# A soft-MoE tail in quarters of the output columns instead of halves

## The chip, the cores and the metric

The kernel runs on one core of a Trainium2 chip. The metric is the device time of one launch, in microseconds (us). TensorE is written PE in the profile (PEld for its weight loads), VectorE DVE, ScalarE ACT, GpSimd POOL, and SP is the engine that here issues all DMAs.

## The reference

A linear-attention block (8 batches, 8 heads, 576 tokens, 64 channels) feeds a soft mixture of experts. The change is in the last stage of the second part, so that part is quoted; `x` is the attention's output, 4608 tokens by 512 columns, with 8 experts of 4 slots each and a hidden width of 1024.

```
logits = x @ phi                              # 4608 x 32
d = softmax of logits over the tokens
slot_input = (d.T @ x).reshape(8, 4, 512)
for e in range(8):
    h = relu(slot_input[e] @ w1[e])           # 4 x 1024
    slot_out[e] = h @ w2[e]                   # second layer, 4 x 512
c = softmax of logits over the 32 slots
return c @ slot_out.reshape(32, 512)          # 4608 x 512, float32
```

All inputs and outputs are float32. The output is 9.44 MB; w1 and w2 are 16.8 MB each.

## The kernel before, in words

The attention part takes most of the time and is the same in both kernels; a planner (class `Plan`) sets the order of its work. Behind it everything that PE does is written out by hand, inside `tc.manual_schedule(engines={PE})`; the other engines take their instructions in the order in which a scheduler puts them.

SP loads the 64 tiles of expert weights (512 KB each, `load_w`, L235) into slots of SBUF as these come free, the 32 tiles of w2 last. They are ordered by half `a` of the output columns: 16 tiles (two for each expert) for columns 0 to 255, then 16 for 256 to 511. Behind the last weights SP issues the output DMAs, in order.

The names of the tail, each with its function:

- `hp` (L810) is the first layer, `hidden`/`picked` apply the ReLU (`hs`, L864 on ACT and L865 on DVE) and turn it around (`psh`, L873) into `sh`, the stationary operand of the second layer.
- `layer2(a, e)` (L907) is the second layer of expert `e` for half `a`: eight matmuls, one for each 128 of the hidden width, each with 32 stationary columns (the 32 slots, those of other experts being zero) and 256 moving columns of w2. Four of them go to four groups of 32 PE columns side by side. The sums of all experts stand in `yp`, one PSUM bank for each half. A float32 matmul shows as two instructions in the trace, so one call makes 16.
- `slots(a)` (letter `s`) copies `yp` to `ys` on DVE; `slots2` (`r`, for the second half `R`) adds up the four groups by one matmul with `rep` (`psy`, L920), and ACT and DVE split the result into a pair of rounded parts, `yr` (L923).
- `combine(i)` (`C`) makes the moving operand of 512 tokens' outputs: four transposes on PE (`psc`, L893), a copy on ACT (L897) and a subtraction on DVE (L898) to `cT[i]`. The first three of nine are made earlier, under the names `psc` L604 and `xT`. `psc` and `psy` share two PSUM buffers (`pd`).
- `output(a, i, yr)` (`o`) makes 512 tokens of a half: two matmuls of 512 moving columns (`pso`, L931), one for each 128 output columns, one evicted by DVE and the other by ACT (L932) into a tile `o`, and one DMA of 512 KB (L933). `pso` rotates over four PSUM banks.

The string `TAIL` sets the order of these on PE, one letter a step; `L` is half an expert of the second half of the columns. All of half 0's second layer stands ahead of `TAIL`, and the nine outputs of half 1 behind it.

Of the kernel before, what the change touches and what calls it, by code (L numbers as in the profile page):

```python
# [9 lines left out]
F32 = mybir.dt.float32  # L10
F32R = mybir.dt.float32r
AF = mybir.ActivationFunctionType
ALU = mybir.AluOpType
# [3 lines left out]
B, H, S, D = 8, 8, 576, 64  # L17
# [11 lines left out]
DM, NE, SPE, FF = 512, 8, 4, 1024  # L29
NS = NE * SPE  # L30
KC = DM // 128
FC = FF // 128
SP, PE, ACT, DVE, POOL = (getattr(mybir.EngineType, n) for n in ("SP", "PE", "Activation", "DVE", "Pool"))
NTT = B * S // 128
DH = DM // 2
# [5 lines left out]
NCT = 3  # L41
# [79 lines left out]

TAIL = "CCLLrLLoLLCoLLCoLLCoLLCoLLoLoLsoRo"


@with_exitstack
def tile_kernel(ctx: ExitStack, tc, xT, vv, w, phi, w1, w2, cst, out):
# [7 lines left out]
    nc = tc.nc  # L136
# [44 lines left out]
    for i in range(NWARM):  # L181
        ps = pmm.tile([128, 512], F32, tag="mm", name="psw")
# [9 lines left out]
    cs = const.tile([128, 257], F32, name="cs")  # L192
    ident = cs[:, 0:128]
    rep = cs[:, 128:256]
    low4 = cs[:, 256:257]
# [23 lines left out]
    keep = [10, 11, 12, 13]  # L219
    order = [j for j in range(nslot[-1]) if j not in keep]  # L220
    wt = []
    wpools = [wpool]

    def slot(j, name, dt=F32):
        return wpools[sum(j >= n for n in nslot)].tile([128, 1024], dt, tag=f"w{j}", name=name)
# [372 lines left out]
    cT = []  # L598
# [39 lines left out]
    for s in range(NK):  # L638
        u, c = divmod(s, NCH)
        bp, h = divmod(u, H)  # L640
        n = bp, c
# [6 lines left out]
        bank = [f"kb{s % 2}"]  # L648
# [8 lines left out]
        bank = [f"qb{s % 2}"]  # L657
# [148 lines left out]
    def layer1(a, kcs):  # L806
        for kc in kcs:
            for n in range(2):
                for e in range(4):
                    nc.tensor.matmul(hp[a][32 * e:32 * e + 32, n], si[:, kc],  # L810
                                     wt[(a * KC + kc) * 4 + e][:, n * 512:(n + 1) * 512],
                                     start=kc == 0, stop=kc == KC - 1, skip_group_check=True)
# [27 lines left out]
    def bank(shape, name):  # L840
        cps.append(cps.pop(0))
        return cps[-1].tile(shape, F32, tag="nm0" if cps[-1] is pmo else "mo", name=name)

    def lastw():
        for c in range(NCH):
            n = NBP - 1, c
            ps = bank([128, CH, NS], "psL")
            turned(lTs.pop(n), ps)
            l = sm.tile([128, CH, NS], F32, tag="ls", name="ls", bufs=3)
            nc.vector.tensor_copy(l, ps)  # L850
            wmax(n, l)
            wsub(n, nc.vector)
            wexp(n)
            wsum(n)
            wdiv(n, nc.vector)

    sh = []
# [4 lines left out]
    def hidden(a):  # L862
        t = slot(keep[a], "hs")
        nc.scalar.activation(t[:, 0:512], hp[a][:, 0], AF.Relu, scale=rs)  # L864
        nc.vector.tensor_scalar(t[:, 512:1024], hp[a][:, 1], rs, 0.0, op0=ALU.mult, op1=ALU.max)  # L865
        return t

    def picked(a, t):
        for i in range(2):
            ps = bank([128, FC // 2, 4, NS], "psh")  # L870
            for c in range(FC // 2):
                o = (FC // 2 * i + c) * 128
                nc.tensor.transpose(ps[:, c].rearrange("p e s -> p (e s)"), t[:, o:o + 128], ident)  # L873
            for e in range(4):
                c0 = (4 * a + e) * SPE
                nc.vector.tensor_copy(sh[a][:, e, FC // 2 * i:FC // 2 * (i + 1), c0:c0 + SPE], ps[:, :, e, c0:c0 + SPE])


    spare = [order[i] for i in range(len(wsrc) - nslot[-1], len(order)) if order[i] < NE * KC]
    gone = [i if i < nslot[-1] else order[i - nslot[-1]] for i in range(NE * KC, NE * (KC + 2))]  # L880
    cws, cts = [], []

    def repeated(i):

        if i % 2:
            cws.append(slot(spare[6 + i // 2 - 1], "cw").rearrange("p (g m) -> p g m", g=2))
        cw = cws[-1][:, 1 - i % 2].rearrange("p (j a s) -> p j a s", a=4, s=NS)
        nc.gpsimd.tensor_copy(cw, call[:, 4 * i:4 * i + 4].unsqueeze(2).broadcast_to([128, 4, 4, NS]))

    def combine(i):  # L890
        ps = pd.tile([128, 4, 128], F32, tag="c", name="psc")
        for j in range(4):
            nc.tensor.transpose(ps[:, j], cws[(i - NCT) // 2][:, 1 - i % 2, j * 128:(j + 1) * 128], ident)  # L893
        if i % 2:
            cts.append(slot(spare[i // 2 - 1], "cT", F32R).rearrange("p (g m) -> p g m", g=2))
        x, ps = cts[-1][:, 1 - i % 2], ps.rearrange("p j m -> p (j m)")
        nc.scalar.copy(x, ps)  # L897
        nc.vector.tensor_tensor(x[64:128], ps[64:128], x[64:128].bitcast(F32), op=ALU.subtract)  # L898
        cT.append(x)


    yp = ph[0].tile([128, 2, 512], F32, tag="h", name="yp")

    def layer2(a, e, cs=range(FC)):
        for c in cs:
            g = 32 * (c % 4)
            nc.tensor.matmul(yp[g:g + 32, a, 0:DH], sh[e // 4][:, e % 4, c],  # L907
                             wt[NE * KC + (a * NE + e) * 2 + c // 4][:, (c % 4) * DH:(c % 4 + 1) * DH],
                             start=(e == 0 and c < 4), stop=(e == NE - 1 and c >= 4), skip_group_check=True)

    def slots(a):
        ys = slot(spare[3 + a], "ys")[:, 0:DH]
        nc.vector.tensor_copy(ys, yp[:, a, 0:DH])
        return ys

    yrs = slot(spare[5], "yr", F32R)

    def slots2(a, ys):
        ps = pd.tile([128, DH], F32, tag="c", name="psy")
        nc.tensor.matmul(ps, rep, ys, start=True, stop=True)  # L920
        yr = yrs[:, DH * a:DH * a + DH]

        yis = [nc.scalar.copy(yr, ps), nc.vector.scalar_tensor_tensor(yr, yr.bitcast(F32), low4, ps, op0=ALU.mult, op1=ALU.add)]  # L923
        return yr, yis[0].ins, yis[-1].ins

    def output(a, i, yr):

        o = slot(gone[i] if a == 0 else (gone[9:16] + keep[0:2])[i], "o").rearrange("p (b t) -> p b t", b=2)
        for b in range(2):
            ps = bank([128, 512], "pso")  # L930
            nc.tensor.matmul(ps, yr[:, b * 128:(b + 1) * 128], cT[i], start=True, stop=True)  # L931
            (nc.scalar.copy if b else nc.vector.tensor_copy)(o[:, b], ps)  # L932
        nc.sync.dma_start(out[a, i], o.rearrange("p b t -> p (b t)"))  # L933

    NO = NTT // 4
    with tc.manual_schedule(engines={PE}):
        layer1(1, range(0, 1))
        lastw()
        layer1(1, range(1, 2))
        picked(0, hidden(0))  # L940
        layer1(1, range(2, KC))
        layer2(0, 0)
        layer2(0, 1)
        picked(1, hidden(1))
        stacks["h"].close()
        pd = ctx.enter_context(tc.tile_pool(name="pd", bufs=2, space=PSUM, reuse_waits="tile"))
        for i in range(NCT, NO):
            repeated(i)
        for e in range(2, NE):
            layer2(0, e)  # L950
        ys = slots(0)
        cs, outs, l2 = iter(range(NCT, NO)), iter(range(NO)), iter(range(2 * NE))
        behind = ExitStack()
        for step in TAIL:
            if step == "L":
                e, i = divmod(next(l2), 2)
                layer2(1, e, range(4 * i, 4 * i + 4))
            elif step == "C":
                combine(next(cs))
            elif step == "o":  # L960
                output(0, next(outs), yr)
            elif step == "s":
                ys = slots(1)
            elif step == "r":
                yr, *_ = slots2(0, ys)
            else:
                yr2, *ins = slots2(1, ys)
                for x in ins:
                    behind.enter_context(tc.issue_after(x))
        behind.close()  # L970
        for i in range(NO):
            output(1, i, yr2)


# [32 lines left out]
```

## Time and profile before

| | us |
|---|---|
| median of 3 runs (355.0 to 357.64) | 356.8 |
| the profiled execution | 356.55 |
| its span, first to last instruction | 354.6 |
| PE busy in the span | 340.3 (96%) |
| DVE, ACT, POOL busy | 261.2, 247.0, 168.8 |
| written to HBM | 9.44 MB |

The profiled execution took 1.95 us more than its span. The tail that the change touches begins at 312.7 us, with the first matmul of the second layer.

### The profile page before, as it was taken

Reading aid. Unit: us, or ns where it says so; the run is one execution under the profiler, and the core shown is the slowest. Engines: PE = TensorE matmul, PEld = TensorE weight load, DVE = VectorE, ACT = ScalarE, POOL = GpSimd, SP = SyncE. Lnnn points to the kernel's source line nnn. Section 1 sums busy time; section 2 is a strip of 40 time slices with the busy share of each in tenths; the row PEclk is TensorE's granted clock in tenths of the full one; section 3 lists DMA queues with packets and bytes.
Section 4 is the critical chain, followed back from the end, with each engine's and each line's share of the span. In section 5 each row is a group of like instructions: output and inputs, shape, how many; then the busy total and the mean of one; then the engine's idle time right before and its main releaser. Section 6 shows DMA issues by size and latency. Waiting matters only on the chain.

```text
span 354.6 us, 16589 instructions
## 1 busy us (share of the span) xinstructions
PE 340.3 (96%) x6901; PEld 277.7 (78%) x6901; DVE 261.2 (74%) x762; ACT 247.0 (70%) x840; POOL 168.8 (48%) x356
## 2 busy tenths in 40 slices
PE   8999999999999989999999999999999999999980
PEld 4899989998898879888888998889899755455440
DVE  1678888888889777889897887997887644614680
ACT  3798899869867978788679878877887351203460
POOL 1546666753473756544747674557475400230000
PEclk9999999999999999999999999999999999999996
DMA  6646567535526655545266565344431998997698
GB/s 211 204 137 204 171 209 242 174 108 205 183 57 217 204 190 168 167 143 190 53 210 226 176 206 166 130 165 127 149 99 28 357 414 312 414 415 323 250 409 350
DMA packets 22074, 74.13 MB, mean 209 GB/s; under 512 B 2928, under 2 KB 3184, under 8 KB 22000
## 3 DMA queue, kind: packets, MB, share of 16 engines
q1 hardware_dynamic: 22000, 73.08, 59.2%
q8 instruction: 54, 0.88, 1.0%
q14 instruction: 20, 0.16, 0.1%
HBM read 63.64 MB, written 9.44 MB: 206 GB/s over the span
## 4 chain that ended last, share of the span: by engine, by line
PE 88%; ACT 5%; DVE 3%; issue 1%; POOL 0%; ACTq 0%; DVEq 0%; POOLq 0%
PE kvp L310 20%; PE psn L367 19%; PE psk L266 12%; PE psq L266 9%; PE psx L700 5%; PE yp L907 4%; PE hp L810 4%; PE psl L412 4%; PE pso L931 2%; PE pss L446 2%; PE psw L183 1%; ACT o L932 1%; PE psc L893 1%; ACT kf L292 1%; ACT mh L344 1%
## 5 line engine op out<-in xcount | busy, mean ns | idle before, releaser
L285 POOL TENSOR_TENSOR vs<-vt,mk 128x390 f32<-128x390 f32 (+3 forms) x128 | 91.8, 729 | 63.3 <-PE kvp L310 25.7
L310 PE MATMUL kvp<-vs,kf 128*64 128x65 f32 (+1 forms) x2304 | 92.4, 229 | 1.1 <-issue 1.1
L367 PE MATMUL psn<-kvs,qf 128*64 128x65 f32 x2304 | 85.1, 224 | 1.2 <-ACT qf L336 0.5
L310 PEld LDWEIGHTS kvp<-vs,kf 128*64 128x64 f32 x2304 | 79.2, 138 | 6.9 <-issue 3.3
L367 PEld LDWEIGHTS psn<-kvs,qf 128*64 128x64 f32 x2304 | 75.8, 138 | 8.9 <-issue 1.6
L266 PE MATMUL psk<-wd,xs 64*128 64x128 f32 x576 | 81.5, 284 | 0.0
L266 PE MATMUL psq<-xs,wd 64*128 64x128 f32 x576 | 81.2, 284 | 0.0
L266 PEld LDWEIGHTS psk<-wd,xs 64*128 64x128 f32 x576 | 69.1, 187 | 8.2 <-issue 3.1
L266 PEld LDWEIGHTS psq<-xs,wd 64*128 64x128 f32 x576 | 69.0, 187 | 2.0 <-ACT qf L336 1.0
L332 ACT ACTIVATE qf<-psq 128x384 f32<-128x384 f32 (+2 forms) x96 | 46.2, 484 | 25.3 <-PE psq L266 13.2
L272 DVE TENSOR_REDUCE mk<-psk 128x3 f32<-128x384 f32 (+2 forms) x96 | 51.5, 542 | 15.3 <-PE psk L266 11.3
L326 DVE TRANSPOSE_TENSOR_REDUCE mt<-psq 128x12 f32<-128x384 f32 (+2 forms) x96 | 53.8, 569 | 7.2 <-ACT qf L336 3.5
L292 ACT ACTIVATE kf<-psk 128x384 f32<-128x384 f32 (+2 forms) x96 | 45.9, 486 | 9.8 <-DVE mk L272 8.3
L402 POOL TENSOR_TENSOR xc<-un,dn 128x192 f32<-128x192 f32 x96 | 47.0, 506 | 11.2 <-DVE dn L394 6.3
L336 ACT ACTIVATE qf<-psq 128x384 f32<-128x384 f32 (+2 forms) x96 | 46.2, 483 | 0.1
L296 ACT ACTIVATE kf<-psk 128x384 f32<-128x384 f32 (+2 forms) x96 | 45.7, 488 | 0.0
L378 DVE TENSOR_TENSOR un<-psn,eq 128x195 f32<-128x195 f32 x96 | 32.7, 346 | 11.4 <-PE psn L367 8.3
L383 DVE TENSOR_TENSOR un<-psn,un 128x195 f32<-128x195 f32 x96 | 32.8, 353 | 1.7
L350 DVE TENSOR_REDUCE eq<-mh 32x9 f32<-32x36 f32 x128 | 26.5, 207 | 8.9 <-ACT mh L344 6.8
L344 ACT ACTIVATE mh<-mt 32x36 f32<-32x36 f32 x128 | 29.2, 228 | 3.6 <-DVE mt L326 2.3
L276 ACT ACTIVATE mk<-mk 128x3 f32<-128x3 f32 (+2 forms) x96 | 19.9, 209 | 4.2 <-DVE mk L272 3.2
L700 PE MATMUL psx<-cs,xc 128*128 128x128 f32 x135 | 19.7, 282 | 0.0
(124 smaller groups left out, 355.4 us busy)
## 6 DMA issues: line engine op xcount, KB each, us to landing
wt<-w SPq DMA_DIRECT2D x64, 512.0 KB, 6.8
xs<-xT SPq DMA_DIRECT2D x32, 576.0 KB, 4.1
vt<-vv SPq DMA_DIRECT2D x32, 325.0 KB, 3.1
out<-o SPq DMA_DIRECT2D x18, 512.0 KB, 3.2
xs<-xT SPq DMA_DIRECT2D x1, 160.0 KB, 3.1
cs<-cst SPq DMA_DIRECT2D x1, 128.5 KB, 3.8
xs<-xT SPq DMA_DIRECT2D x1, 128.0 KB, 3.1
wd<-w SPq DMA_DIRECT2D x1, 64.0 KB, 2.7
```

The source lines that it names most:

```text
L266: nc.tensor.matmul(ps, a, b, start=True, stop=True)
L272: nc.vector.tensor_reduce(km[s][:, 2, 0:n], kx[s][:, 0:n], axis=AX, op=ALU.max, apply_absolute_value=True)
L285: nc.gpsimd.tensor_tensor(x[:, :, o:o + n], v[:, t:t + n].unsqueeze(1).broadcast_to([128, 2, n, 65]), em[:, 0:2, i:i + n].unsqueeze(3).bro ...
L292: nc.scalar.activation(kf[s][:, 1, 0:n], kx[s][:, 0:n], AF.Exp, scale=-1.0)
L296: nc.scalar.activation(kf[s][:, 0, 0:n], kx[s][:, 0:n], AF.Exp)
L310: nc.tensor.matmul(ps[f:f + FE // 2, pn, o:o + m], k2[:, pn, i, f:f + FE // 2], v2[:, pn, 65 * i:65 * i + m], start=(t == 0 and pn == 0), ...
L326: nc.vector.tensor_reduce(mts[u].rearrange("p r j -> p j r")[:, t:t + n], qx[s][:, 0:n * 128].rearrange("p (j t) -> p j t", t=32), axis=AX ...
L332: nc.scalar.activation(qf[s][:, 0, 0:n], qx[s][:, 0:n], AF.Exp)
L336: nc.scalar.activation(qf[s][:, 1, 0:n], qx[s][:, 0:n], AF.Exp, scale=-1.0)
L367: nc.tensor.matmul(ps[64 * f:64 * f + 64, j, pn], q2[:, pn, o + 64 * f:o + 64 * f + 64], kv[:, pn, b2], start=True, stop=True)
L402: nc.gpsimd.tensor_tensor(xc[bp, c][:, :, h * D:(h + 1) * D], un[u][:, t, 0:64], dn[u][:, t].unsqueeze(2).broadcast_to([128, CH, 64]), op= ...
L700: nc.tensor.transpose(ps[:, o], xc[n][:, j, kc * 128:(kc + 1) * 128], ident)
```

## The change: what it does

The second layer and the outputs go by quarters of 128 columns (`q` = 0 to 3). A call of `layer2(q, e)` has as many matmuls as before, with 128 moving columns each, so the second layer has 512 matmul instructions where it had 256. Quarters 0 and 1 both read the 16 weight tiles of the first half, quarters 2 and 3 those of the second; `yp` holds two quarters at a time. `L` is now a whole expert of a quarter. There are four `s` and four `r` steps, with 128 columns each. `output(q, i, yr)` makes one matmul of 512 tokens and one eviction, by DVE where `q + i` is even and by ACT where it is odd; two of them share a tile `o` and a DMA of 512 KB, and the ninth goes alone with 256 KB, so there are 20 output DMAs instead of 18. The output array has the shape (4, 128, 4608): a DMA writes pieces of 4 KB (2 KB for the ninth) that lie 18 KB apart, where before it wrote one block of 512 KB. The host turns the array round in both kernels.

```diff
-TAIL = "CCLLrLLoLLCoLLCoLLCoLLCoLLoLoLsoRo"
+TAIL = "sCCrLLLooCLooCLoCLoCLooLosLrLLLoooLLoooLLsoooLrLLLoooLLLLsoooroooooooooooo"
...
-    def layer2(a, e, cs=range(FC)):
-        for c in cs:
-            g = 32 * (c % 4)
-            nc.tensor.matmul(yp[g:g + 32, a, 0:DH], sh[e // 4][:, e % 4, c],
-                             wt[NE * KC + (a * NE + e) * 2 + c // 4][:, (c % 4) * DH:(c % 4 + 1) * DH],
+    def layer2(q, e):
+        for c in range(FC):
+            g, o = 32 * (c % 4), c % 4 * DH + q % 2 * 128
+            nc.tensor.matmul(yp[g:g + 32, q % 2, 0:128], sh[e // 4][:, e % 4, c],
+                             wt[NE * KC + (q // 2 * NE + e) * 2 + c // 4][:, o:o + 128],
...
-    def output(a, i, yr):
-        o = slot(gone[i] if a == 0 else (gone[9:16] + keep[0:2])[i], "o").rearrange("p (b t) -> p b t", b=2)
-        for b in range(2):
-            ps = bank([128, 512], "pso")
-            nc.tensor.matmul(ps, yr[:, b * 128:(b + 1) * 128], cT[i], start=True, stop=True)
-            (nc.scalar.copy if b else nc.vector.tensor_copy)(o[:, b], ps)
-        nc.sync.dma_start(out[a, i], o.rearrange("p b t -> p (b t)"))
+    def output(q, i, yr):
+        if i % 2 == 0:
+            os[q] = slot(gone[(5 * q + i // 2) % 16], "o").rearrange("p (b t) -> p b t", b=2)
+        ps = bank([128, 512], "pso")
+        nc.tensor.matmul(ps, yr, cT[i], start=True, stop=True)
+        (nc.scalar.copy if (q + i) % 2 else nc.vector.tensor_copy)(os[q][:, i % 2], ps)
+        if i % 2 or i == NO - 1:
+            n = i % 2 + 1
+            nc.sync.dma_start(out[q, :, 512 * (i + 1 - n):512 * (i + 1)], os[q][:, 0:n].rearrange("p b t -> p (b t)"))
...
-    o = nc.dram_tensor("out", (2, NTT // 4, 128, 2 * 512), F32, kind="ExternalOutput").ap()
+    o = nc.dram_tensor("out", (4, 128, B * S), F32, kind="ExternalOutput").ap()
```

Three places of the program show what moved. First PE where the second layer's first part ends (`wt` is a weight tile, `yp` the second layer, `psc` a combine step, `psy` the adding up, `pso` an output). Before:

```order
L907 MATMUL yp<-wt_6708,sh 32x256 x4
L893 MATMUL psc<-cs,cw 128x128 x8
L907 MATMUL yp<-wt_6710,sh 32x256 x4
L907 MATMUL yp<-wt_6712,sh 32x256 x4
L920 MATMUL psy<-ys,cs 128x256
L907 MATMUL yp<-wt_6714,sh 32x256 x4
L907 MATMUL yp<-wt_6716,sh 32x256 x4
L931 MATMUL pso<-xT,yr 128x512 x2
```

Now:

```order
L907 MATMUL yp<-wt_6708,sh 32x128 x4
L893 MATMUL psc<-cs,cw 128x128 x8
L920 MATMUL psy<-ys,cs 128x128
L907 MATMUL yp<-wt_6355,sh 32x128 x4
L907 MATMUL yp<-wt_6357,sh 32x128 x4
L907 MATMUL yp<-wt_6359,sh 32x128 x4
L907 MATMUL yp<-wt_6458,sh 32x128 x4
L907 MATMUL yp<-wt_6460,sh 32x128 x4
L907 MATMUL yp<-wt_6462,sh 32x128 x4
L934 MATMUL pso<-xT,yr 128x512 x2
```

`psy` stands right behind the two combine steps, where an expert stood between them, and quarter 1 starts again at the first weight tile, 6355.

The second place is new: PE between quarters 1 and 2, with what each instruction waits for.

```order
L907 MATMUL yp<-wt_6708,sh 32x128 x4
L934 MATMUL pso<-cT,yr 128x512 [waits DVE_49]
L907 MATMUL yp<-wt_6710,sh 32x128 [waits DMAHW5_49,DVE_49]
L907 MATMUL yp<-wt_6710,sh 32x128 x3
L907 MATMUL yp<-wt_6712,sh 32x128 [waits DMAHW6_49]
L907 MATMUL yp<-wt_6712,sh 32x128 x3
L920 MATMUL psy<-ys,cs 128x128 [waits PE_49]
```

The first matmul of quarter 2 (tile 6710) waits for DVE, whose copy `ys` of quarter 1 is queued behind the eviction of that `pso`.

The third place is PE's end. Before:

```order
L907 MATMUL yp<-wt_6740,sh 32x256 x4
L931 MATMUL pso<-cT,yr 128x512 x2
L920 MATMUL psy<-ys,cs 128x256
L931 MATMUL pso<-cT,yr 128x512 x2
L931 MATMUL pso<-xT,yr 128x512 x6
L931 MATMUL pso<-cT,yr 128x512 x12
```

Now:

```order
L907 MATMUL yp<-wt_6738,sh 32x128 x4
L907 MATMUL yp<-wt_6740,sh 32x128 x4
L934 MATMUL pso<-cT,yr 128x512 x3
L920 MATMUL psy<-ys,cs 128x128
L934 MATMUL pso<-cT,yr 128x512 x3
L934 MATMUL pso<-xT,yr 128x512 x3
L934 MATMUL pso<-cT,yr 128x512 x6
```

Behind the last matmul of the second layer there were 22 output matmuls, and there are 15 now.

## Rows read from the trace of the kernel before

**Rows 1.** The page, the span in 40 slices: tenths of PE's busy time, of its granted clock and of the DMA engines' busy time.

```profile
PE   8999999999999989999999999999999999999980
PEclk9999999999999999999999999999999999999996
DMA  6646567535526655545266565344431998997698
```

**Rows 2.** Busy time by stretch of the tail: stretch, its length, then busy us and (x instructions) of PE, PEld, DVE, ACT and POOL, the granted clock, the DMA engines' busy share and GB/s.

```profile
312.70:324.60 11.90, 11.90 (x182) 6.77 (x174) 3.76 (x13) 2.13 (x4) 3.39 (x6) 1.00 1.01 412
324.60:337.00 12.40, 12.40 (x131) 6.10 (x127) 7.62 (x11) 5.99 (x11) 0.00 (x0) 1.00 0.58 235
337.00:341.20 4.20, 3.62 (x16) 1.89 (x13) 3.47 (x7) 2.73 (x6) 0.00 (x0) 1.00 0.97 398
341.20:353.70 12.50, 3.79 (x13) 1.74 (x12) 4.54 (x7) 3.82 (x8) 0.00 (x0) 0.81 0.98 401
```

**Rows 3.** The queue of SP, three of its DMAs: start, us of the issue, what. The last weight, the ninth output and the last one.

```profile
317.24 0.33 SPq L235 DMA_DIRECT2D wt<-w  x1
...
339.86 0.33 SPq L933 DMA_DIRECT2D out<-o  x1
...
348.80 1.14 SPq L933 DMA_DIRECT2D out<-o  x1
```

**Rows 4.** The same three DMAs among the DMA issues, each in a stretch of its own: KB and us from issue to landing.

```profile
wt<-w SPq DMA_DIRECT2D x1, 512.0 KB, 9.9
...
out<-o SPq DMA_DIRECT2D x1, 512.0 KB, 2.6
...
out<-o SPq DMA_DIRECT2D x1, 512.0 KB, 4.9
```

**Rows 5.** The chain that ended last, from the second layer's first matmul on, in order of time: start, us, what.

```profile
312.88 1.73 PE yp L907 x32
314.61 1.02 PE psh L873 x8
315.63 5.32 PE yp L907 x96
320.95 1.02 PE psc L893 x8
321.97 1.00 PE yp L907 x16
322.97 0.67 PE psy L920 x2
...
326.35 0.59 PE psc L893 x4
326.93 0.47 PE pso L931 x2
...
334.57 0.66 PE pso L931 x2
335.23 0.57 PE yp L907 x8
...
338.36 0.33 ACT yr L923
...
338.71 0.49 DVE yr L923
```

**Rows 6.** Matmuls of 128 moving columns in groups of 32 PE columns, in the tail's earlier part: first the chain's row, then two of the timeline of PE (start, us, what).

```profile
303.66 0.66 PE psc L604 x24
...
293.35 0.83 PE L604 MATMUL psc<-cs,call 128*32 128x128 f32 x22
...
333.50 1.07 PE L907 MATMUL yp<-wt,sh 128*32 128x256 f32 x16
```

**Rows 7.** The timeline of DVE at the second ReLU: start, us, what.

```profile
313.75 0.75 DVE L865 TENSOR_SCALAR hs<-hp,rs 128x512 f32<-128x512 f32 x1 [3.35 <-ACT hs L864]
```

**Rows 8.** Groups by line and shape from 300 us on: count, busy us, mean ns of one, idle time before them.

```profile
L932 DVE COPY o<-pso 128x512 f32<-128x512 f32 x18 | 12.1, 689 | 5.1 <-PE pso L931 4.7
L932 ACT COPY o<-pso 128x512 f32<-128x512 f32 x18 | 10.3, 588 | 5.7 <-PE pso L931 5.6
...
L898 DVE TENSOR_TENSOR cT<-psc,cT 64x512 fp32r<-64x512 f32 x6 | 4.1, 694 | 0.9 <-ACT cT L897 0.7
...
L897 ACT CAST cT<-psc 128x512 fp32r<-128x512 f32 x6 | 3.4, 587 | 11.8 <-PE psc L893 11.8
...
L913 DVE COPY ys<-yp 128x256 f32<-128x256 f32 x2 | 0.8, 424 | 5.1 <-PE yp L907 4.9
```

**Rows 9.** The timelines of PE, DVE and ACT at one output: start, us, what. The pair of output matmuls, and its two evictions.

```profile
334.50 0.73 PE L931 MATMUL pso<-cT,yr 128*128 128x512 f32 x2
...
335.03 0.69 DVE L932 COPY o<-pso 128x512 f32<-128x512 f32 x1 [0.25 <-PE pso L931]
...
335.26 0.58 ACT L932 COPY o<-pso 128x512 f32<-128x512 f32 x1 [1.06 <-PE pso L931]
```

More of the change, by code (lines that the diff above doesn't have):

```diff
@@ L909, in layer2, with slots, slots2 @@
                              start=(e == 0 and c < 4), stop=(e == NE - 1 and c >= 4), skip_group_check=True)
-    def slots(a):
-        ys = slot(spare[3 + a], "ys")[:, 0:DH]
-        nc.vector.tensor_copy(ys, yp[:, a, 0:DH])
+    def slots(q):
+        ys = slot(spare[3 + q % 2], "ys")[:, 0:128]
+        nc.vector.tensor_copy(ys, yp[:, q % 2, 0:128])
         return ys
     yrs = slot(spare[5], "yr", F32R)
-    def slots2(a, ys):
-        ps = pd.tile([128, DH], F32, tag="c", name="psy")
+    def slots2(q, ys):
+        ps = pd.tile([128, 128], F32, tag="c", name="psy")
@@ L920, in slots2 @@
         nc.tensor.matmul(ps, rep, ys, start=True, stop=True)
-        yr = yrs[:, DH * a:DH * a + DH]
-        yis = [nc.scalar.copy(yr, ps), nc.vector.scalar_tensor_tensor(yr, yr.bitcast(F32), low4, ps, op0=ALU.mult, op1=ALU.add)]
-        return yr, yis[0].ins, yis[-1].ins
-    def output(a, i, yr):
-        o = slot(gone[i] if a == 0 else (gone[9:16] + keep[0:2])[i], "o").rearrange("p (b t) -> p b t", b=2)
-        for b in range(2):
-            ps = bank([128, 512], "pso")
-            nc.tensor.matmul(ps, yr[:, b * 128:(b + 1) * 128], cT[i], start=True, stop=True)
-            (nc.scalar.copy if b else nc.vector.tensor_copy)(o[:, b], ps)
-        nc.sync.dma_start(out[a, i], o.rearrange("p b t -> p (b t)"))
@@ L935, in tile_kernel @@
-    NO = NTT // 4
+        yr = yrs[:, 128 * q:128 * q + 128]
+        return yr, [nc.scalar.copy(yr, ps).ins,
+                    nc.vector.scalar_tensor_tensor(yr, yr.bitcast(F32), low4, ps, op0=ALU.mult, op1=ALU.add).ins]
+    NO = NTT // 4
+    os = {}
+    def output(q, i, yr):
[7 more added lines that the diff above has]
+            nc.sync.dma_start(out[q, :, 512 * (i + 1 - n):512 * (i + 1)], os[q][:, 0:n].rearrange("p b t -> p (b t)"))
@@ L950, in tile_kernel @@
             layer2(0, e)
-        ys = slots(0)
-        cs, outs, l2 = iter(range(NCT, NO)), iter(range(NO)), iter(range(2 * NE))
+        cs, l2 = iter(range(NCT, NO)), iter((q, e) for q in range(1, 4) for e in range(NE))
+        ys, outs = [], []
         behind = ExitStack()
@@ L955, in tile_kernel @@
             if step == "L":
-                e, i = divmod(next(l2), 2)
-                layer2(1, e, range(4 * i, 4 * i + 4))
+                layer2(*next(l2))
             elif step == "C":
@@ L960, in tile_kernel @@
             elif step == "o":
-                output(0, next(outs), yr)
+                output(*outs.pop(0))
             elif step == "s":
-                ys = slots(1)
-            elif step == "r":
-                yr, *_ = slots2(0, ys)
-            else:
-                yr2, *ins = slots2(1, ys)
-                for x in ins:
-                    behind.enter_context(tc.issue_after(x))
+                ys.append(slots(len(ys)))
+            else:
+                q = len(ys) - 1
+                yr, ins = slots2(q, ys[q])
+                outs += [(q, i, yr) for i in range(NO)]
+                if q == 3:
+                    for x in ins:
+                        behind.enter_context(tc.issue_after(x))
         behind.close()
-        for i in range(NO):
-            output(1, i, yr2)
 def kernel(q, k, v, w_phi, moe_phi, moe_w1, moe_w2):
@@ L1003 @@
     r = run_bass_kernel_spmd(nc, [arrays], core_ids=[0])
-    y = np.asarray(r.results[0]["out"]).reshape(2, NTT // 4, 128, 2, 512)
-    return c(y.transpose(1, 4, 0, 3, 2)).reshape(B * S, DM)
+    return c(np.asarray(r.results[0]["out"]).reshape(DM, B * S).T)
```

## The prediction

> **What bounds the kernel now.** I read the span in slices first: PE is busy nearly everywhere, its clock is granted in full up to the last slice, and the DMA engines are full in the last slices alone [rows 1]. The tail by stretches then shows three limits in turn [rows 2]. Up to 324.6 us PE works without a gap and the DMA engines are full too, with the last weights. From 324.6 to 337.0 PE is still without a gap (12.40 of 12.40), but the DMA engines run at 0.58: outputs come out of PE slower than they could be stored. From 341.2 on it is the other way round, PE 3.79 of 12.50 and DMA 0.98.
>
> The queue of SP says what sets the end. The ninth output was issued at 339.86 [rows 3] and landed 2.6 us later [rows 4], the last was issued at 348.80 and landed 4.9 later, at 353.7. So nine DMAs of 512 KB landed in 11.24 us, 1.25 each: that is the rate of a full queue, and 2.6 us the time of one that finds it empty. The span ends 0.9 behind the last landing. The end is therefore a sum: when the queue ran dry for the last time, 2.6, and 1.25 for each 512 KB after that. Before, the last dry spell is that around PE's second `psy`, with `yr` on ACT and DVE behind it (0.33 and 0.49) [rows 5].
>
> A floor follows too: the last weight was issued at 317.24 and landed 9.9 later, at 327.1 [rows 3, 4]. 18 times 1.25 behind it is 349.6, 4.1 us under 353.7. So the change can win 4.1 us at most, and it wins them only where the outputs keep the queue filled.
>
> **The change part by part.** *Second layer.* Before, 96 instructions took 5.32 [rows 5], 0.222 for four, which run side by side; 8 in a run of their own took 0.57, so a run costs 0.13 at its edges. At 128 columns the nearest row is another matmul of the same kind, 32 stationary columns and 128 moving ones: 24 in 0.66 [rows 6], 0.110 for four. An expert of a quarter is four fours, 0.44. All of the second layer then is 128 fours, 14.1 us, against 64 times 0.222, 14.2: the streaming costs the same. The upper end is 22 in 0.76 (293.35 to 294.11, where another matmul starts) [rows 6], 0.138 for four, and 3.6 us more in all. The lower end is half of 0.222, no gain. I take 0.110, the row without a change of kind before it. There are 15 runs where there were 11: 0.5 us more.
>
> *`psy`.* Four of 128 columns instead of two of 256 at 0.67 [rows 5]. A narrow one lies between half of that and the whole; I take 0.42.
>
> *Outputs.* 36 matmuls and 36 evictions, as before. Two output matmuls took 0.47 behind `psc` and 0.66 behind `yp` [rows 5]: 0.235 each and 0.19 at the edges, so one costs 0.43 and three 0.90. What changes is how many PE does ahead of its last expert: 24 instead of 16, counting those up to the last `psy`.
>
> *The path on PE to the last dry spell.* The queue now dries for the last time while PE does three and then four experts of quarter 3, so the date wanted is the issue of the DMA behind these (output 3 of quarter 2, evicted by ACT). From 312.88 [rows 5]:
>
> two experts 0.88, to 313.76. The second four `psh` read what DVE writes until 314.50 [rows 7], so PE waits there and is through at 315.0 (before 315.63). Six experts 2.77, to 317.77; two combines 1.02, to 318.79. Now `psy` stands right behind them and needs one of the two buffers that they hold: the first combine's transposes end at 318.36, ACT copies for 0.59 and DVE subtracts for 0.69 [rows 8], with hand-overs 319.75, a wait of 0.95. Behind it on PE are queued the experts of quarter 1. `psy` to 320.15, three experts 1.45 to 321.6. In the next stretch a pair of outputs with a combine costs 0.59 + 0.47 = 1.06 [rows 5] and a single one 0.83: two of each, five experts at 0.57, a pair 0.66 and a single 0.43, 7.7 in all, to 329.3.
>
> There the first matmul of quarter 2 waits for DVE's `ys`. DVE first evicts the output before it: the matmul starts at 328.9, an eviction follows 0.53 after such a start [rows 9] and lasts 0.69, and `ys` is about 0.29 (0.424 at 256 columns, 0.689 at 512 [rows 8]): 330.45, a wait of 1.1. Behind it stand quarter 2 and the `psy` that lets quarter 1's outputs out.
>
> Expert 0.57 and `psy` 0.42, to 331.45; three experts 1.45, outputs 0.90, two experts 1.01, outputs 0.90, two experts 1.01, outputs 0.90, to 337.6; expert and `psy` 0.99, to 338.6; three experts and three outputs 2.35, to 340.95; four experts 1.89, to 342.85. The next output matmul is evicted 0.53 later for 0.59: **the DMA is issued at 344.0**. The one before it was issued at 341.4 and landed at 344.0, so the queue is dry indeed.
>
> *The sum.* Behind 344.0 come 2.6 and then 14 blocks of 256 KB, seven times 1.25: 355.35. Before it was 353.7. That is 1.65 us later, and 356.55 + 1.65 = **358.2**; the profiled execution lies 0.25 under the median of the runs. The point from which the change wins is an issue at 342.35. Put otherwise: at 344.0 both kernels have landed 5.24 MB, ten DMAs before, and two quarters and a DMA now. The head start of the first quarter (a first issue near 323, against 326) is spent, since the weights hold the queue to 327.1, and since PE then has longer runs of experts between the outputs.
>
> *The pieces in HBM.* They are 4 KB in both kernels, now 18 KB apart; no row shows such a store. I take the same 1.25. If the four DMAs of 256 KB cost as much as a whole one, the two behind the dry spell add 1.25 together. The other way there is no reason for a gain.
>
> **The rivals.** *A matmul of 128 columns costs more than half of one of 256.* At 0.138 for four, PE is 3.6 us later at 342.85 and the end with it: 361.8. For it speaks that PE has twice as many instructions here; against it the row of 24, in which the moving columns alone set the pace, and that the clean rows show no wait. The Trainium skill, page "TensorE: Matmul & The Clock Gate", section "Back-to-back issue gap", gives for a lasting stream of weight loads and matmuls some 81 ns at 128 columns and 131 ns at 512, so narrow ones are far from proportional. On a straight line through its figures 128 columns cost 0.83 of 256; the second layer would be some 9 us longer by that (an estimate from that page), and the kernel at about 367. The 24 in 0.66 speak against the rule here, where four column groups run side by side. I give this rival 0.14; the kernel is slower by over 1% from about 0.127 for four on.
>
> *The stores are slower.* Pieces 18 KB apart, or the small DMAs, cost a tenth more of 22.5 us plus the 1.25 above: 3.5 on top, 361.7. Only the full queue at the end would show it. 0.08.
>
> *The outputs do fill the queue.* Then the idle 0.42 of the stretch from 324.6 to 337.0 [rows 2] is used, and the end comes up to 4.1 us earlier: 352.4. It needs the last issue of the sum 1.65 us earlier to break even and 4 or more to be felt. Without the three waits at `psh`, `psy` and `ys` (0.2, 0.95 and 1.1) it is 2.25 earlier, which gives 355.9; the rest would have to come out of matmuls whose durations are in the rows. 0.10 for more than 1% faster.
>
> **How the numbers follow.** No difference that a measurement of this kernel can tell (1%, 3.6 us) is the forecast: 0.68, at 358.2, with its own range from 355.9 (no waits) to 359.5 (the small DMAs). Faster by over 1% gets 0.10, slower by over 1% 0.22, the first two rivals together. The range must leave out 0.2 at most: from 354.5, half way into the third rival, to 361.5, just short of the first two.
>
> **What would show it.** In the profile after: the second layer's fours at 0.11; a wait of about a microsecond ahead of the first narrow `psy`, and another at quarter 2's first expert; outputs issued from 323 on; the DMA engines idle in part from 331 to 346; PE's last expert ending near 343 instead of 337; from about 345 on a full queue, at 1.25 for 512 KB. I am wrong if the fours take over 0.12, if the two waits are absent, or if the full stretch at the end runs at another rate than 420 GB/s.

## The result, and the profile after

| | before | after |
|---|---|---|
| median of the runs compared | 355.84 us (354.84 to 357.64) | 358.72 us (357.64 to 360.66) |
| profiled execution | 356.55 | 360.62 |
| its span | 354.6 | 358.8 |
| tail: from the second layer's first matmul to the span's end | 312.70 to 354.61, 41.92 | 314.14 to 358.84, 44.70 |

The ratio is 1.008, with a 95% interval of 1.0051 to 1.011. The changed kernel is slower, by 2.9 us by the medians, and this is under the 1% that the prediction called no difference, though the interval reaches just beyond it. The ratios here and below are taken over runs in the faster of the program's two states alone, so that a ratio isn't always the quotient of the medians beside it. What lies ahead of the tail is the same program in both kernels, and its length differs by up to 3.4 us from one profiled execution to another, of whichever kernel. So in what follows kernels are compared by their tail, and times "behind the tail's start" count from the second layer's first matmul. The tail is 2.78 us longer, within 0.1 of the difference of the medians, 2.88. Each tail is that of one profiled execution; where two kernels have the same steps in the same order, they agree within 0.1 us (44.70 and 44.71, 40.39 and 40.47 below).

The page of the profile after, in the form of [rows 1], with the row of PE's busy time and the two queues that fetch instructions:

```profile
PE 343.5 (96%) x7161; PEld 285.3 (80%) x7161; DVE 262.0 (73%) x766; ACT 247.6 (69%) x842; POOL 168.9 (47%) x356
...
PE   8999999999999989999999999999999999989990
...
PEclk9999999999999999999999999999999999999997
DMA  6555567535526655555365565445232999997677
...
q8 instruction: 56, 0.92, 1.1%
q14 instruction: 21, 0.17, 0.1%
```

The clock is granted in full up to the last slice, as before. In the DMA row the last slices read 7677 where they read 7698 before: there are more slices in which the queue isn't full. The stretches, in the form of [rows 2]:

```profile
312.70:324.60 11.90, 10.79 (x224) 8.00 (x220) 4.22 (x14) 2.59 (x6) 3.39 (x6) 1.00 1.03 418
...
324.60:337.00 12.40, 11.42 (x202) 7.79 (x195) 6.78 (x11) 5.18 (x11) 0.00 (x0) 1.00 0.60 242
337.00:346.00 9.00, 9.00 (x178) 6.64 (x176) 4.86 (x9) 3.40 (x7) 0.00 (x0) 1.00 0.80 320
346.00:358.00 12.00, 3.83 (x11) 1.58 (x10) 4.25 (x8) 3.81 (x8) 0.00 (x0) 0.87 0.87 352
```

PE now has gaps, about one microsecond in each of the first two stretches, where it had none in [rows 2]. From 337 to 346 it works without one, and the DMA engines are at 0.80: the last dry spell, which before was over at 341.2. The gaps by name are in the chain that ended last, in order of time (start, us, what), which answers to [rows 5]:

```profile
315.18 0.77 DVE hs L865
...
315.99 0.66 PE psh L873 x4
316.65 2.76 PE yp L907 x96
...
320.03 0.59 ACT cT L897
320.62 0.02 issue
320.65 0.70 DVE cT L898
321.35 0.04 issue
321.39 0.49 PE psy L920 x2
321.88 1.45 PE yp L907 x48
...
331.28 0.69 DVE o L935
331.97 0.21 DVE ys L913
332.18 0.04 issue
332.22 0.64 PE yp L907 x16
332.87 0.42 PE psy L920 x2
333.29 1.45 PE yp L907 x48
...
342.77 1.88 PE yp L907 x64
344.65 0.90 PE pso L934 x3
```

Twice the chain leaves PE and comes back: at 320.03 to 321.35 for the combine's eviction by ACT and DVE, behind which the first `psy` gets its buffer, and at 331.28 to 332.18 for an output's eviction and `ys`, which stands behind it on DVE. The waits ahead of `psy` and of quarter 2's first expert are 0.97 and 0.98 us (timeline of PE):

```profile
321.39 0.49 PE L920 MATMUL psy<-ys,cs 128*128 128x128 f32 x2 [0.97 <-DVE cT L898]
...
332.22 0.64 PE L907 MATMUL yp<-wt,sh 128*32 128x128 f32 x16 [0.98 <-DVE ys L913]
```

PE's last expert ends at 344.65, and the DMA behind it is the one that the prediction called the last to find the queue dry. In the queue of SP (start, us of the issue, what) and among the DMA issues (KB, us to landing), in the form of [rows 3, 4]:

```profile
345.73 0.33 SPq L938 DMA_DIRECT2D out<-o  x1
...
352.83 1.12 SPq L938 DMA_DIRECT2D out<-o  x1
```

```profile
out<-o SPq DMA_DIRECT2D x1, 512.0 KB, 2.6
...
out<-o SPq DMA_DIRECT2D x1, 256.0 KB, 5.1
```

It did find the queue dry (2.6 us) but for one engine's share: the DMA ahead of it, issued at 343.19, landed only at 347.12, and from 345.4 to 346.5 the engines moved 23 GB/s where a full queue moves some 420. The DMA of 345.73 landed at 348.37. The 14 blocks of 256 KB behind it landed by 357.89, in 9.53 us, where seven times 1.25 is 8.75.

So the balance is: issued 31.59 us behind the tail's start instead of 27.16 for the ninth output before, 4.43 later; from there to the last landing 12.16 instead of 13.85, 1.69 less; with 0.04 at the span's end, 2.78.

### The profile page after: what moved, and what is told of

Read it like the earlier page. It is cut to its first block, busy times and chain, and to the rows that moved or that the text cites. A ratio compares the mean times of both kernels' runs of the same rounds, so it can differ in the third digit from the quotient of the medians.

```text
span 358.8 us, 17124 instructions
## 1 busy us (share of the span) xinstructions
PE 343.5 (96%) x7161; PEld 285.3 (80%) x7161; DVE 262.0 (73%) x766; ACT 247.6 (69%) x842; POOL 168.9 (47%) x356
## 4 chain that ended last, share of the span: by engine, by line
PE 88%; ACT 5%; DVE 4%; issue 2%; POOL 0%; ACTq 0%; DVEq 0%; POOLq 0%
PE kvp L310 20%; PE psn L367 18%; PE psk L266 12%; PE psq L266 9%; PE psx L700 5%; PE yp L907 4%; PE hp L810 4%; PE psl L412 4%; PE pso L934 3%; PE pss L446 2%; PE psw L183 1%; ACT kf L292 1%; ACT mh L344 1%; PE psw L620 1%; PE pss L544 1%
```

## The experiments

Each median and ratio is taken beside runs of the kernel before on the same chip. The expectations stand as they were written before each run.

**Without the waits.** The changed kernel with the first `psy` behind two experts, and `ys` of quarter 1 ahead of an output:

```
-TAIL = "sCCrLLLooCLooCLoCLoCLooLosLrLLLoooLL..."
+TAIL = "sCCLLrLooCLooCLoCLoCLooLsoLrLLLoooLL..."
```

> The order string alone is changed: two experts of quarter 1 stand ahead of the first psy (they stood behind it), and the copy ys of quarter 1 stands ahead of that quarter-0 output which it stood behind. That takes both waits of about 1.0 us off PE. Theory (the end is the last dry spell of the DMA queue, which PE's path dates): the DMA of quarter 2's outputs 2 and 3, issued 31.45 us after the second layer's first matmul in the changed kernel, is issued 1.7 to 2.0 us earlier, and the whole kernel takes 1.7 to 2.0 us less, about 1.003 of the kernel before. Rival (the lost time is in the stores at the end): the issue comes earlier, the end hardly does, 1.006 to 1.008.

The median was 357.75 us, ratio to before 1.004 (1.0012 to 1.0067). The DMA in question was issued at 341.85:

```profile
341.85 0.33 SPq L938 DMA_DIRECT2D out<-o  x1
```

That is 30.13 us behind the tail's start instead of 31.59, 1.47 earlier (1.7 to 2.0 had been expected), and the tail is 43.24, 1.46 shorter. The end follows this one issue one for one. The first wait is gone. The second is down to 0.17 of PE's time, since `ys` still stands behind an eviction (the chain):

```profile
327.40 0.44 DVE o L935
327.84 0.17 issue
328.01 0.29 DVE ys L913
328.30 0.04 issue
328.35 0.65 PE yp L907 x16
```

The waits were what the prediction took them for, and they aren't all of the loss: 1.3 us of tail remain against the kernel before.

**Contiguous blocks in HBM.** The changed kernel, with each DMA's block in one piece of HBM, in the order of the DMAs, instead of 4 KB pieces 18 KB apart.

> The changed kernel with every output DMA writing one contiguous block of HBM, as the kernel before did; the host puts the blocks together. Theory: the place of the pieces does not matter, same time as the changed kernel, 1.008 of before, and still 9.5 us from the landing of quarter 2's outputs 2 and 3 to the last landing. Rival (pieces 18 KB apart are slower to store): that stretch shrinks from 9.5 to 8.75 us or less and the kernel to 1.006.

358.24 us, ratio 1.0075 (1.0046 to 1.0103); the tail is 44.71, as in the changed kernel, and the full stretch behind the DMA that found the queue dry took 9.57. Where the pieces lie costs nothing.

**Single DMAs.** The changed kernel with 36 DMAs of 256 KB, one for each output matmul, in place of 20.

```
-        if i % 2 or i == NO - 1:
-            n = i % 2 + 1
-            nc.sync.dma_start(out[q, :, 512 * (i + 1 - n):512 * (i + 1)], ...)
+        nc.sync.dma_start(out[q, :, 512 * i:512 * (i + 1)], os[q][:, i % 2])
```

> The changed kernel with one DMA of 256 KB (pieces of 2 KB) for each output, 36 in all, where 16 of 512 KB and 4 of 256 KB stood. Theory: in a full queue 256 KB takes half of 512 KB, so the stretch from quarter 2's output 3 on stays at 9.5 us or less and the kernel at 1.005 to 1.010 of before. Rival (a DMA of 256 KB costs more than its half; the changed kernel's two in that stretch seem to have cost some 0.4 us extra each): 14 in that stretch would cost 14 x 0.63 + 14 x 0.4 = 14.4 us, and the kernel 5 us more than the changed one, 1.02.

358.17 us, ratio 1.0072 (1.0043 to 1.0101), tail 44.29, 0.41 shorter. In a full queue one of 256 KB landed 0.63 us behind the last, half of 1.25: small DMAs have no price of their own here. Two of them did take 1.04 and 1.12 us, at 351.6 and 352.7. The missing 0.8 us at the end is thus neither the shape nor the place of the stores; it sat in one spot.

**Narrow matmuls in the kernel before.** Each second-layer matmul of 256 columns as two of 128, nothing else.

```
+            for b in range(2):
...
-                nc.tensor.matmul(yp[g:g + 32, a, 0:DH], ...
+                nc.tensor.matmul(yp[g:g + 32, a, b * 128:b * 128 + 128], ...
```

> The kernel before with one part of the change alone: each second-layer matmul of 256 columns is made as two of 128, in groups of four side by side; order, outputs and DMAs are those of before. Theory: four narrow ones take 0.110 us, so the second layer streams for 14.1 instead of 14.2 us and the time stays within 0.3% of before. Rival (a matmul of 128 columns costs more than half of one of 256): at 0.138 for four the kernel is 3.6 us longer, 1.010; by a straight line through the skill's figures some 9 us.

359.33 us, ratio 1.006 (1.0027 to 1.0094), tail 44.01. Neither side was right. Four narrow ones take 0.109 us here too, and from the first `psy` to the second the tail is as long as before (14.71 us, before 14.63). Of the 2.09 us that the tail lost, 1.87 lie ahead of the first `psy`, and 1.49 of them are one gap in the long run of half 0 (timeline of PE):

```profile
318.78 2.24 PE L909 MATMUL yp<-wt,sh 128*32 128x128 f32 x73
322.50 1.08 PE L909 MATMUL yp<-wt,sh 128*32 128x128 f32 x31 [1.49 <-issue]
```

PE waits 1.49 us for nothing that the profile names. A run that narrows half 1 alone, whose experts have other work between them, tells whether narrow matmuls or the long run are at fault:

> The kernel before with the second half's second-layer matmuls alone as two of 128 columns. Theory (a matmul of 128 columns costs half of one of 256, and what the run with both halves narrow lost was one stall of 1.49 us in the long unbroken run of narrow matmuls of the first half): no stall, fours of 0.109 us, tail 41.9 us as in the kernel before, within 0.3. Rival (narrow matmuls cost in broken runs too, at the edges or in some other place): tail 42.6 us or more, half of what the run with both halves narrow lost.

This is one profiled execution (356.52 us), with no further runs. Tail 41.98, as before within 0.06; no such gap. So narrow matmuls cost half of wide ones, and the gap came only in the long run of them. That it is PE's supply of instructions is likely (twice as many in the same time, with the weights filling the DMA engines), and wasn't tried by itself.

**The order of the quarters.** By the sum that the first run had borne out, another order of the same steps should win: more of quarter 1 ahead of the combines, combines in pairs, and outputs in fours and sixes as soon as their `yr` is there.

```
+TAIL = "CCsLLLLLrLCCooooLLCCsoooLLLLrooooooLLLLLsoooorLLooooLLooooLLLsoorooooooooo"
```

> The changed kernel with another order of its last steps and nothing else: more of quarter 1 ahead of the combines, combines two at a time, outputs in fours and sixes as soon as a quarter's yr is there. Theory (what the change lost is the order: the queue runs dry while PE does experts, and the end follows the issue behind the last dry spell one for one): by the same durations worked along this order, PE waits nowhere for more than 0.3 us, the first output is issued about 13 us after the second layer's first matmul, the DMA behind the last dry spell about 22.5 us after it, ten DMAs of 512 KB are left behind that, the tail is 39.6 us against 44.7 of the changed kernel and 41.9 of the kernel before, and the time about 353.5 us, ratio 0.993 to the kernel before. Rival (quarters cost by themselves: more blocks, more hand-overs, the stall behind an instruction fetch): the tail stays over 42 us, the time at 356 us or above.

354.98 us, ratio 0.9962 (0.9936 to 0.9988): 0.4% faster than before, and the tail is 2.96 shorter than in the changed kernel, 41.74. So the changed kernel had lost by its order. But it is 2.1 us over the sum, and only 0.18 under the tail of the kernel before. The ratio says some 1.4 us; the rest of that lies ahead of the tail, where the program is the same, and no run shows why.

**Halves in another order.** The same question for the kernel before.

```
-TAIL = "CCLLrLLoLLCoLLCoLLCoLLCoLLoLoLsoRo"
+TAIL = "CCLLLLLrLLLoooCCooLLLCCooLLLLLsoRo"
```

> The kernel before, in halves, with another order of its last steps and nothing else. Theory (halves are bound by the second half's own length: its outputs can't start before all eight experts of 256 columns are through): the order can win about 1.5 us, by bringing the second psy from 24.9 to about 23.9 us behind the second layer's first matmul; tail 40.4 us, time 354.4 us, ratio 0.996. Rival (the order alone is what counts, whatever the pieces): as fast as the two kernels in quarters with an order of their own, 352.3 to 353.5 us.

356.56 us, ratio 0.9998 (0.9965 to 1.0031), tail 41.84: no gain. The second `psy` did come at 23.6 us instead of 24.9. But the first output, issued at 328.50 into a queue that the weights had left at 327.10, took 4.9 us to land instead of 2.6, and from there the queue was full to the end: 17 landings in 21.1 us. Between its issue and its landing, at 329.58, PE's queue of instructions moved one packet of 16 KB, which took 1.75 us. The order had been expected to win 1.5 us, so this run leaves open what halves could gain by it without that packet.

**A half and two quarters.** The first half of the columns in one piece, as before, the second as two quarters (the hybrid).

```
+TAIL = "sLLrCLooCCooLLCooCCLLLsoorLLoooLLLooooLLLsooroooooooooo"
+WIDTHS, FIRST = (2, 1, 1), (0, 2, 3)
...
+        a, w = FIRST[q], WIDTHS[q] * 128
...
+            nc.tensor.matmul(yp[g:g + 32, q % 2, 0:w], sh[e // 4][:, e % 4, c],
```

> The first half of the columns in one piece as in the kernel before, the second half as two quarters, in an order of its own. Theory (the end is the last dry spell and what is left behind it; the first half needs no splitting, since the weights hold the queue until then, and the quarters are wanted for the last half alone): last dry spell at about 21 us after the second layer's first matmul, the queue nearly always full behind it, tail 38.3 us against 41.9 of the kernel before, time about 352.3 us, ratio 0.99. Rival (each split costs what the changed kernel lost): tail 42 us or more, time 356 us or more.

355.87 us, ratio 0.9971 (0.9941 to 1.0001), tail 40.39: 1.5 under the kernel before, 2.1 over the sum. This run put the rows of the last two quarters one block too early in HBM; the next has them in their place.

> The first half of the columns in one piece, the second as two quarters, in the order of the hybrid run before, with each quarter's rows put at their own place in HBM (the run before put quarter 2 and 3 one row block too early). Theory: the place costs nothing, so the tail is again 40.4 us (40.1 to 40.7), against 41.9 of the kernel before, and the time 1.5 us under the kernel before in comparable runs, ratio 0.996. Rival (the gain in the tail is bought back ahead of it, or is chance): ratio 1.0.

**354.68 us, ratio 0.9946 (0.9920 to 0.9972), tail 40.47.** It has the lowest ratio of these kernels, 0.5% under the one before. The ratio's interval overlaps that of the quarters in their new order, but its tail is 1.27 us shorter than theirs. Its stretches show why, and what is left (columns as in [rows 2]):

```profile
324.90:328.00 3.10, 3.10 (x43) 2.27 (x42) 2.84 (x5) 2.26 (x6) 0.00 (x0) 1.00 0.87 338
328.00:331.00 3.00, 2.53 (x54) 2.05 (x55) 2.91 (x5) 2.12 (x4) 0.00 (x0) 1.00 1.00 386
331.00:349.00 18.00, 11.98 (x172) 7.99 (x161) 9.38 (x17) 6.94 (x14) 0.00 (x0) 0.92 1.01 398
349.68:350.58 0.90, 0.00 (x0) 0.00 (x0) 0.00 (x0) 0.00 (x0) 0.00 (x0) 0.50 0.12 46
```

Its last weight landed at 324.92, and from 328 on the DMA engines are busy throughout: the dry spell of [rows 2] is gone. In the last 0.9 us before the last packet of a store they are at 0.12, two of 16.

**One DMA engine that comes late.** The same last 0.9 us in the kernel before and in the changed one:

```profile
352.50:353.40 0.90, 0.00 (x0) 0.00 (x0) 0.00 (x0) 0.00 (x0) 0.00 (x0) 0.50 0.75 305
```

```profile
356.63:357.53 0.90, 0.00 (x0) 0.00 (x0) 0.00 (x0) 0.00 (x0) 0.00 (x0) 0.50 0.08 27
```

Before, the engines end within 0.3 us of each other. In the changed kernel 15 of them are done by 0.8 us before the last, and the last store waits for that one: its last nine packets end one behind another, 0.08 us apart. The trace doesn't number the engines, so that the late one is the one that carried a packet of instructions, as is held below, is an inference from the times. In the changed kernel, and in the three above that keep its full stretch at the end, the landings fall behind at the moment at which a packet of 8 KB passes on the queue q14 of instructions. In the changed kernel it is this one (the DMA queues from 351.0 to 351.6 us: packets, MB, share):

```profile
q14 instruction: 1, 0.01, 3.2%
```

It passes just behind the last evictions of ACT and DVE (350.23 and 349.95); in the kernel before the packet comes at 355.7, behind the last landing. To see whether it is the cause, the changed kernel got 32 short instructions more on DVE and on ACT at its start, which moves the packet.

```
+    pad = const.tile([32, 16], F32, name="pad")
+    for i in range(32):
+        nc.vector.memset(pad[:, 0:8], 0.0)
+    for i in range(32):
+        nc.scalar.copy(pad[:, 8:16], pad[:, 0:8])
```

> The changed kernel with 32 memsets on DVE and 32 small copies on ACT added at the program's start, whose results nobody reads. Theory (the last 0.8 us of the changed kernel is one DMA engine that is late because it fetched 8 KB of instructions for ACT or DVE at 351.2, in the middle of the last stores): the fetch comes 32 instructions of that engine earlier, near 340 where the queue runs dry, no fetch is left behind 346, the last stretch has all 16 DMA engines end together, and the tail falls by 0.8 us, from 44.7 to 43.9. Rival (the slow end is in the stores' own number or shape, the fetch only a coincidence): the tail stays at 44.7 within 0.2.

The packet moved to 330.35, and none of that queue came behind it. The last 0.9 us:

```profile
354.88:355.78 0.90, 0.00 (x0) 0.00 (x0) 0.00 (x0) 0.00 (x0) 0.00 (x0) 0.50 0.84 323
```

The late engine is gone, as the theory has it. The tail fell by half of what it had forecast, to 44.29 (the DMA behind the dry spell was issued at 31.59 us again, so all of it lies in the full stretch, 9.11 us instead of 9.53). The median of the whole kernel, 359.32 us, ratio 1.0075 (1.0044 to 1.0106), doesn't tell it from the changed kernel. The other half went into slower blocks: those of 512 KB landed 1.29 to 1.34 us apart instead of 1.25, and the packets of 4 KB took 164 ns on average in that stretch, where they took 159 in the kernel before and in the changed one and 160 in the hybrid. The tile of 64 bytes a partition, which moves the tiles behind it in SBUF, is new there, but whether it is the cause stays open: in a kernel further down that has it too (the one with 73 matmuls) the packets also took 164 ns on average, and the blocks landed 1.24 apart. So this run changes two things at once, the moment of the packet and the place of the tiles.

In the hybrid PE's own packets of 16 KB are the larger part. They were moved in two runs:

```
-NWARM = 11
+NWARM = 8
...
+    for i in range(73):
+        g = 32 * (i % 4)
+        nc.tensor.matmul(ps[g:g + 32, 0:32], warm[:, 0:32], warm[:, 0:32], ...)
```

> The same hybrid with small instructions added at the program's start, whose results nobody reads: 73 small matmuls in place of three long ones on PE, 32 memsets on DVE and 32 copies on ACT. They change nothing in the tail but the moments at which the engines fetch their next instructions. Theory (what the tail lost against its sum is one DMA engine of the 16 that carries a fetch of instructions of 16 KB while the other 15 move stores, and the last store waits for it): the fetches move from 334.4 and 339.4 to about 329 and 336, where the queue runs dry or nearly so, and the tail falls by about 1 us, to 39.4 (39.0 to 39.9). Rival (the stretched landings have another cause, in the order or the stores themselves): the tail stays at 40.4 within 0.2.

> The hybrid with 60 more small matmuls at PE's start (63 in place of three long ones) whose results nobody reads, and nothing else: no new tile in SBUF and nothing on ACT and DVE, unlike the run with the shift before, in which the packets of 4 KB took 164 ns instead of 159 and a third fetch of PE's instructions fell into the last stores. Theory (the last store waits for the DMA engine that carried a fetch of PE's instructions): PE's fetches come 120 instructions earlier, at about 14 and 22 us after the second layer's first matmul instead of 20.4 and 25.4, both where the queue is dry or nearly so, and none behind them; the tail falls from 40.5 to between 38.7 and 39.5 (a fetch of 8 KB for another engine stays where it is). Rival (the fetch is not what holds the last store): the tail stays at 40.5 within 0.2. The time: 1 to 1.8 us under the hybrid by the theory, ratio to the kernel before 0.990 to 0.993; by the rival 0.9946.

The first, which has the pad as well, came to 357.38 us, ratio 1.0026 (0.9997 to 1.0056), tail 41.40; the second, with 63 small matmuls and no pad, to 356.31, ratio 0.9974 (0.9943 to 1.0006), tail 41.37. Both were slower than the hybrid, where 1 us less and more was expected: the packets didn't come where they were reckoned (at 14 and 22 us; with 63 matmuls they came at 11.3, 21.7 and 28.0), so two still fell into the full stretch, as in the hybrid. In the second they put the landings back by 3.1 us together, against 2.2 in the hybrid, which agrees with the 0.9 us by which its tail is longer. They are of use for all that. From `TAIL` on the three kernels are one program, and in each of them a landing is late where a packet of 16 KB passes, wherever that is:

| | packet, us behind the tail's start | it took | landing before and behind it | instead of 1.25 |
|---|---|---|---|---|
| hybrid | 20.4 | 0.93 | 331.29, 334.39 | 3.10 |
| | 25.4 | 0.96 | 338.12, 339.76 | 1.64 |
| with 73 matmuls | 21.6 | 0.94 | 335.39, 338.29 | 2.90 |
| | 28.9 | 0.93 | 344.32, 346.57 | 2.25 |
| with 63 matmuls | 21.7 | 1.11 | 334.37, 337.27 | 2.90 |
| | 28.0 | 1.75 | 342.24, 344.94 | 2.70 |

In the run with 63 matmuls no landing but these two is over 1.5 us behind the one before it from 334 on, and its last 0.9 us are those of one engine (the window, then a row of the DMA queues from 340.9 to 341.3):

```profile
352.34:353.24 0.90, 0.00 (x0) 0.00 (x0) 0.00 (x0) 0.00 (x0) 0.00 (x0) 0.50 0.06 23
```

```profile
q8 instruction: 1, 0.02, 27.3%
```

Not every packet does it. In the quarters in their new order, in both runs of the hybrid and in that with 63 matmuls, a packet of 8 KB on q14 passes in the full queue too (at 343.99, 348.16, 345.21 and 347.33 us), and no landing up to the end is more than 0.04 us late behind it. In all four a packet of 16 KB had put a landing back in the full queue before that, so an engine that was late by more may have hidden a second one; no run shows it.

What wasn't reached is the other end: a kernel with no such packet in its full stretch, and so the 38.3 to 38.7 us that the sums give. That the whole 2 us would come back then is an inference.

## Why the prediction was right

It named 358.2 us and no difference by more than 1%; the median is 358.72. That the two lie within 0.5 us is in part luck: 358.2 stands on the profiled execution of the kernel before, 356.55, and the runs compared have a median of 355.84. The difference that it forecast is 1.65 us, the measured one 2.78 in the tail and 2.88 by the medians. The mechanism, a last dry spell dated by PE's path and a full queue behind it, is what the runs showed; two of its terms were too short. Its steps in turn:

- **What sets the end** (last dry spell, 2.6, 1.25 for each 512 KB): right. Moving one issue by 1.47 us moved the end by 1.46, and a queue that no longer dries gave a faster kernel. The small DMAs cost half of a whole one, and the pieces 18 KB apart nothing, as taken.
- **Second layer**: right. 0.109 us for four (16, 32, 48, 64 and 96 instructions in 0.57, 1.01, 1.45, 1.88 and 2.76, so 0.0274 each and 0.13 at the edges). The rival of 0.138 is out. The Trainium skill, page "TensorE: Matmul & The Clock Gate", section "Back-to-back issue gap", gives a lasting stream 81 ns a matmul at 128 columns and 131 ns at 512, by which narrow ones cost far more than their share. The traces don't agree for these, four side by side (0.109 against 0.222 us). What no step had is the stall of 1.49 us in a long run of narrow ones; it came in the kernel before with narrow matmuls, not in the changed one.
- **`psy`**: 0.42 taken, 0.42 measured where nothing holds it up (332.87).
- **The waits**: 0.2, 0.95 and 1.1 forecast, and the last two measured at 0.97 and 0.98, each behind the instruction that was named.
- **The date of the last dry spell**: its 344.0 is 31.3 us behind the start of the tail at 312.70, and 31.59 was measured, 0.3 later. The step that was short is `psh`, by 0.2: the ReLU on DVE ended 1.8 us behind the tail's start in both kernels, as taken, but the four transposes behind it took 0.66, not half of eight, and PE was through at 2.51 us behind the tail's start, not at 2.3.
- **Issue at 323 and PE's end near 343**: in the profiled execution 324.65 and 344.65. It began the tail 1.44 us later; counted from there, both are within 0.4.
- **The full stretch at 1.25**: wrong by 0.78 us. A block costs what it did, but one of 16 engines was late by about as much, and the sum had no term for that. Two errors, 0.3 and 0.8, had the same sign; they make up the difference between 1.65 and 2.78, and stayed within the range, 354.5 to 361.5.
- **The rivals**: "the outputs do fill the queue" fell for this kernel, on the waits and on the order. By the prediction's sum the three waits were worth more than the whole loss (355.9 without them, under the kernel before); the run without the first and most of the second won 1.46 us in the tail and stayed 1.3 above the kernel before, since the loss was 2.78 and not 1.65. The two rivals on the slow side are out.

## What to carry to other kernels

When stores come out at the end, write the time as the issue behind the last dry spell, plus its latency, plus the rate times what is left; splitting the work finer pays only if the order then fills the earlier dry spells, and here the split in its first order cost 2.8 us, and another order of the same steps took 3.0 back. Count what the split makes every queue wait for: two waits of a microsecond, each behind an eviction, were foreseeable from the rows. When a full queue ends later than its bytes explain, look at how many DMA engines are still busy in the last microsecond, and for packets of instructions in the stretch ahead.

## What the runs showed of the hardware

- Instructions share the DMA engines with the data. The page of before has

```profile
PE 340.3 (96%) x6901; PEld 277.7 (78%) x6901; DVE 261.2 (74%) x762; ACT 247.0 (70%) x840; POOL 168.8 (48%) x356
...
q8 instruction: 54, 0.88, 1.0%
```

so 13,802 weight loads and matmuls came in 54 packets of 16 KB, and the 14,322 of after in 56: 256 a packet in both. In the tails one took 0.88 to 1.77 us, and the store that was then in the queue landed up to 2.3 us late (4.91 us behind its issue instead of 2.6, in the halves in another order). Why it was late by more than the packet took isn't shown. In the changed kernel the packet of 1.77 us at 342.64 was made good in the dry spell behind it. In a queue that is full to the end it isn't, so more instructions for the same work can have a price that PE's busy time doesn't show.
- In the two runs with a tile of 64 bytes a partition more in SBUF the packets of 4 KB took 164 ns on average in the full queue, in the others 159 to 160. In one of the two the stores landed more slowly, in the other not, so the cause and what it costs stay open.
